# Sums of a folded Fourier transform on TensorE: eight 32-row, 64-column tiles of the array instead of four of 32 rows and 128 columns

## The chip, the cores and the metric

The kernel runs on one core of one Trainium2 chip. The metric is the device time of one execution in microseconds (us); runs are compared by their median. The profile is one execution of the program, recorded by the hardware profiler. Its engines: PE is the matmul side of TensorE and PEld its weight loads (a matmul keeps one operand, the weights, in the array and streams the other through it), DVE is VectorE, ACT is ScalarE, POOL is GpSimd, SP is SyncE, which only issues DMAs here.

## What is computed

The reference takes `x` of 8 batches, 3008 positions and 256 features, applies a Fourier transform along the positions and then the features, keeps the real part, and feeds every row to a gated feed-forward block with a sigmoid gate:

```
X = np.fft.fft(x, axis=1)
X = np.fft.fft(X, axis=2)
x = X.real.astype(np.float32).reshape(B * S, D)          # 24064 rows of 256
gate = 1.0 / (1.0 + np.exp(-(x @ w_gate)))               # w_gate, w_val: 256 x 1536
val = x @ w_val
return (gate * val @ w_out).astype(np.float32)           # w_out: 1536 x 256
```

All of it is in float32.

## The kernel before

**Stages.** The transform along the features is merged into the weights of the first two products (`merge`, lines 410 to 421). The transform along the positions is made per batch as sums over positions against tables of cosines and sines. Its two results per batch, `pk` and `qk` (128 features by 1505 frequencies), go through the feed-forward block in chunks of 252 frequencies: the matmuls `pf` (lines 774 to 792), the gate on ACT and DVE (lines 794 to 818), sums on POOL (line 824), the matmuls `po` (lines 857 to 896) and the way out (`finish`, line 898). The main loop (line 1151) runs over 8 batches x 6 chunks x 12 tiles of the hidden dimension. The order of everything is written out by hand: `at`, `mid`, `gap` and `spare` are lists that say behind which step of the main loop each piece of the next batch's transform stands.

**The transform of a batch.** Batch 0 uses whole columns of 128 rows (`half`, line 595). Batches 1 to 7 are folded further: by the symmetries of cosine and sine the positions are added and subtracted until a sum runs over a quarter of the rows. What is left are four groups of at most 32 rows, kept in the four quarters of the 128 partitions (`TILES`, line 198: a group `g`, a parity `par` and the first partition `lo`).

**`quarter(b, blk)`, lines 620 to 644**, makes the sums of one block of one batch. It runs 14 times: batches 1 to 7, blocks 1 and 0, from the list `mid` (lines 1093 and 1141). It takes four PSUM banks (`sum`, one for each group `t`). For each of two results (`what`), two parts (`part`) and three slices of rows (`q`), it calls `mm` for the four groups in turn: 48 calls. The weights of a call are 32 rows (31 at the end of some groups) by 128 columns of the folded input; the operand that is streamed is 32 rows by 95 columns (`NQ4`, line 197) of one of the tables `e4`, `r4` and `j4`. Each group starts on a partition of its own, so its call uses its own 32 rows of the array, and writes its own bank, at one of four ranges of 95 columns. Within a range the three slices `q` are added up in PSUM. `mm` (line 132) is a plain matmul with `start` and `stop` flags; the first call of a bank has `start`. All matmuls have line 133 in the profile, that of this helper; they are told apart by the tile they write: `sum` for these, `pf`, `po` and others for the rest. One float32 call of `mm` shows as two weight loads and two matmuls.

**Behind the sums**, ACT copies the four banks out, two copies a bank (line 644), and DVE makes the end results of them later (`quarter_ends`, line 646). The banks of `sum` are those of `po` (tags `po1` to `po4`), so the next matmuls of `po` in these banks wait for the copies. In the main loop `back` (line 1164) stands right ahead of the next matmuls after a `quarter`.

**Another user of parts of the array** is `e_sums` (lines 696 to 735): its matmuls `pe` have 128 rows and one or seven columns of weights, and write partitions 0, 32, 64 and 96 of one bank, so four of them use different columns of the array.

## Time and profile before

| | |
|---|---|
| median of 3 runs | 1908.67 us (1908.12 to 1909.44) |
| the profiled execution | 1909.15 us, span 1907.4 us |
| granted TensorE clock | 1.000 of full speed |
| busy PE, PEld | 1895.6 us, 1756.6 us |
| busy DVE, ACT, POOL | 1520.6, 1353.2, 1543.4 us |
| matmuls `pf`, two kinds | 4608, mean 376 ns each |
| matmuls `po`, two main kinds | 5528, mean 305 and 307 ns each |
| matmuls `sum` | 1344, median 270 ns each, and as many weight loads, median 187 ns |
| ACT copies of the sums (line 644) | 112, median 368 ns |

The span goes from the first to the last instruction; the time of the execution has some 1.7 us around it. Matmuls are pipelined: one lasts from its start to its last result, and the next can start long before that, so durations of one do not add up to busy time, and a busy PE is not one at its peak. In a timeline, neighbouring instructions of one kind are merged into a row: start, duration of all together, engine, line, kind, shapes and how many. A shape such as `32*128 32x95` says 32 rows and 128 columns of the array, and an operand of 32 partitions by 95 elements. In the rows by group, the numbers behind the first bar are busy time in us and the mean duration of one in ns; those behind the second, idle time of the engine ahead of them and what ended it. The chain that ended last is followed back from the last instruction: at each step to what released it, or to the instruction ahead of it on its engine.

### The profile page before, as it was taken

The numbers are of one execution on the slowest core, as the hardware profiler recorded it, in microseconds if no ns is written. First come the engines' busy times: TensorE is split into PE (matmuls) and PEld (weight loads), VectorE is DVE, ScalarE is ACT, GpSimd is POOL, SyncE is SP. The second block draws the span as 40 slices with busy tenths as digits, with TensorE's granted clock in tenths as the row PEclk, the third lists the DMA queues.
The fourth block names the chain that finished last, engine by engine and source line by source line (L and its number), as shares of the span: only waits on it lengthen the run. The fifth ranks groups of instructions, "written<-read, shape, count | busy, mean of one in ns | idle before, by whom it ended". The sixth has DMA issues, their size and how long they took to land.

```text
span 1907.4 us, 36057 instructions
## 1 busy us (share of the span) xinstructions
PE 1895.6 (99%) x11836; PEld 1756.6 (92%) x11836; DVE 1520.6 (80%) x3375; ACT 1353.2 (71%) x3235; POOL 1543.4 (81%) x2733
## 2 busy tenths in 40 slices
PE   8999999999999999999999999999999999999999
PEld 5788999999999999999999999999999999999998
DVE  7678888878979778897788878888788777977775
ACT  4777777777777777777777777677767777777775
POOL 2489879987999779997799878999789986877770
PEclk9999999999999999999999999999999999999999
DMA  8446221212022121211211212122120110010001
GB/s 315 120 134 80 71 89 51 72 33 81 21 64 54 31 87 32 62 41 37 89 39 48 45 39 81 40 52 58 30 74 17 36 37 15 15 25 17 15 18 30
DMA packets 197333, 109.33 MB, mean 57 GB/s; under 512 B 134823, under 2 KB 188818, under 8 KB 195354
## 3 DMA queue, kind: packets, MB, share of 16 engines
q1 hardware_dynamic: 196568, 106.50, 21.1%
q8 instruction: 95, 1.56, 0.3%
q14 instruction: 92, 0.75, 0.1%
q10 hardware_dynamic: 546, 0.51, 0.1%
q0 software_dynamic: 32, 0.00, 0.0%
HBM read 71.24 MB, written 47.87 MB: 62 GB/s over the span
## 4 chain that ended last, share of the span: by engine, by line
PE 94%; DMA 2%; SPq 1%; POOL 1%; ACT 1%; DVE 0%; issue 0%; ACTq 0%; POOLq 0%
PE pf L133 49%; PE po L133 41%; PE sum L133 2%; DMA rtab<-in_stab_dram 1%; PE ps L133 1%; POOL sf L824 1%; DMA st<-in_stab_dram 1%; SPq L206 1%; DMA raw<-in_moe_w_val_dram 0%; PE od L133 0%; POOL x L507 0%; SPq L192 0%; SPq L375 0%; PE pe L133 0%; PE ev L133 0%
## 5 line engine op out<-in xcount | busy, mean ns | idle before, releaser
L824 POOL TENSOR_TENSOR sf<-h,sf 128x168 f32<-128x168 f32 (+1 forms) x1104 | 621.0, 582 | 79.5 <-DVE h L818 75.9
L824 POOL TENSOR_TENSOR sf<-h 128x168 f32<-128x168 f32 (+1 forms) x920 | 519.3, 584 | 159.8 <-DVE h L818 158.0
L133 PE MATMUL pf<-qk,G 128*128 128x252 f32 (+1 forms) x2304 | 583.4, 376 | 0.9 <-ACT ae L787 0.8
L133 PE MATMUL pf<-pk,G 128*128 128x252 f32 (+1 forms) x2304 | 582.7, 376 | 0.0
L772 ACT ACTIVATE pf<-ek,ge 128x252 f32<-128x252 f32 (+1 forms) x1142 | 538.2, 471 | 23.2 <-DMA ge<-G 3.0
L133 PE MATMUL po<-sf,wf 128*128 128x168 f32 (+1 forms) x2944 | 508.3, 305 | 0.0
L787 ACT ACTIVATE ae<-pf 128x504 f32<-128x504 f32 (+1 forms) x576 | 338.8, 588 | 218.7 <-PE pf L133 217.2
L133 PEld LDWEIGHTS pf<-pk,G 128*128 128x128 f32 x2304 | 435.9, 190 | 53.3 <-ACT pf L772 1.5
L133 PE MATMUL po<-h,wf 128*128 128x168 f32 (+2 forms) x2584 | 461.3, 307 | 0.0
L133 PEld LDWEIGHTS po<-sf,wf 128*128 128x128 f32 x2944 | 453.4, 190 | 8.0
L818 DVE TENSOR_TENSOR h<-pf,z 128x252 f32<-128x252 f32 (+1 forms) x576 | 240.4, 417 | 274.0 <-ACT pf L815 270.5
L802 DVE TENSOR_TENSOR z<-ae,pf 128x504 f32<-128x504 f32 (+1 forms) x576 | 384.6, 668 | 83.1 <-ACT h L801 79.1
L908 DVE TENSOR_TENSOR c<-c 128x168 f32<-128x168 f32 (+1 forms) x920 | 438.7, 500 | 3.3
L133 PEld LDWEIGHTS pf<-qk,G 128*128 128x128 f32 x2304 | 410.6, 190 | 32.3 <-ACT ae L787 2.1
L133 PEld LDWEIGHTS po<-h,wf 128*128 128x128 f32 x2584 | 410.4, 190 | 17.8 <-issue 0.9
L801 ACT ACTIVATE h<-pf 128x252 f32<-128x252 f32 (+1 forms) x576 | 216.9, 376 | 146.3 <-PE pf L133 129.0
L815 ACT ACTIVATE pf<-z 128x252 f32<-128x252 f32 (+1 forms) x576 | 214.3, 372 | 116.4 <-DVE h L814 114.5
L814 DVE TENSOR_TENSOR h<-h,pf 128x252 f32<-128x252 f32 (+1 forms) x576 | 232.9, 404 | 0.0
L824 POOL TENSOR_TENSOR sf<-sf 128x168 f32<-128x168 f32 (+1 forms) x184 | 101.7, 553 | 14.4
L824 POOL TENSOR_TENSOR sf<-sf,h 128x168 f32<-128x168 f32 (+1 forms) x184 | 110.1, 598 | 0.0
L891 ACT COPY c<-po 128x504 f32<-128x504 f32 (+1 forms) x138 | 78.5, 569 | 0.0
L918 DVE STREAM_TRANSPOSE os<-c 128x256 f32<-128x256 f32 x188 | 76.5, 427 | 0.1
(158 smaller groups left out, 876.4 us busy)
## 6 DMA issues: line engine op xcount, KB each, us to landing
x<-xr SPq DMA_DIRECT2D x14, 1536.0 KB
out_dram<-os SPq DMA_DIRECT2D x376, 56.0 KB
xr<-in_xf_dram SPq DMA_DIRECT2D x105, 128.0 KB
x<-x SPq DMA_DIRECT2D x112, 96.0 KB
xr<-in_xf_dram SPq DMA_DIRECT2D x14, 384.0 KB
ek<-ed SPq DMA_DIRECT2D x40, 126.0 KB
out_dram<-os SPq DMA_DIRECT2D x288, 7.0 KB
xr<-in_xf_dram SPq DMA_DIRECT2D x21, 124.0 KB
```

The costliest lines, as they stand in the source:

```text
L133: nc.tensor.matmul(o, l, r, start=start, stop=stop, skip_group_check=True)
L772: nc.scalar.activation(PF[i][:, g], EK[i // NFT], AF.Copy, scale=ge[:, g, f : f + 1])
L787: nc.scalar.activation(AP[i], PF[i], AF.Copy, scale=2.0)
L801: nc.scalar.activation(H[p][:, fh, 0:n], PF[i][:, 0], AF.Sigmoid)
L802: nc.vector.tensor_tensor(z[:, :, ::-1], AP.pop(i), PF[i], op=ALU.subtract)
L814: nc.vector.tensor_tensor(h[:, fh, 0:n], h[:, fh, 0:n], pf[:, 1], op=ALU.mult)
L815: nc.scalar.activation(pf[:, 0], z[:, 0], AF.Sigmoid)
L818: nc.vector.tensor_tensor(h[:, fh, n:], pf[:, 0], z[:, 1], op=ALU.mult)
L824: nc.gpsimd.tensor_tensor(block(p, dst), block(p, a), block(p, b), op=(ALU.subtract, ALU.add)[op])
L891: (nc.vector.tensor_copy if t == 1 or t == 3 else nc.scalar.copy)(C[0][:, 3 * t * R : 3 * (t + 1) * R], PO[t][:, 0 : 3 * R])
L908: nc.vector.tensor_tensor(t[:, dst * R : (dst + 1) * R], *v, op=(ALU.subtract, ALU.add)[op])
L918: nc.vector.transpose(os_[0][0][:, s, 0:nb, h, :], t[:, c0 : c0 + nb * TB])
```

## The change

In `quarter`, each of the 48 calls becomes two. The first takes the weights' columns 0 to 63 and writes partitions 0 to 63 of the bank, the second takes columns 64 to 127 and writes partitions 64 to 127. Both stream the same 95 columns of the same table. The `start` and `stop` flags are as before, in each half. Nothing else is changed: the same banks, copies and places in the order.

```diff
                         c0 = (2 * what + 1 - part) * NQ4
-                        mm(ps[t][:, c0 : c0 + NQ4], W[b, blk][what][rows, w], tab,
-                           what == part == q == 0, q == N3 - 1)
+                        for at_ in (slice(0, HP), slice(HP, P)):
+                            mm(ps[t][at_, c0 : c0 + NQ4], W[b, blk][what][rows, w, at_], tab,
+                               what == part == q == 0, q == N3 - 1)
```

`HP` is 64 and `P` is 128. The halves of one group have the same rows of the array and different columns of it; with four groups they make eight tiles of 32 rows and 64 columns.

## The prediction, made before the result was known

> **What bounds the kernel now.** I read the busy shares first, then the chain that ended last, then the same chain around one of the stretches that the change touches.

> ```profile
> PE 1895.6 (99%) x11836; PEld 1756.6 (92%) x11836; DVE 1520.6 (80%) x3375; ACT 1353.2 (71%) x3235; POOL 1543.4 (81%) x2733
> ...
> PE 94%; DMA 2%; SPq 1%; POOL 1%; ACT 1%; DVE 0%; issue 0%; ACTq 0%; POOLq 0%
> PE pf L133 49%; PE po L133 41%; PE sum L133 2%; DMA rtab<-in_stab_dram 1%; PE ps L133 1%; POOL sf L824 1%; DMA st<-in_stab_dram 1%; SPq L206 1%; DMA raw<-in_moe_w_val_dram 0%; PE od L133 0%; POOL x L507 0%; SPq L192 0%; SPq L375 0%; PE pe L133 0%; PE ev L133 0%
> ```

> TensorE (PE) is the bound: 94% of the chain, no other engine over 81% busy. The sums of `quarter` are 2% of the chain, about 40 us, so that is all the change can work on. The chain in order of time near 220 us shows that a `quarter` is on it as a whole, between its neighbours on PE:

> ```profile
> 219.29 1.70 PE pf L133 x8
> 220.99 2.86 PE sum L133 x96
> 223.85 1.75 PE po L133 x10
> ```

> A microsecond saved or lost inside a `quarter` is therefore one in the total. There are 1344 matmuls of `sum` in the trace, 96 in each: 14 quarters (7 batches, two blocks). The code makes 48 calls of `mm` in each, so one float32 call is two loads and two matmuls.

> **What a quarter costs, and why.** The timeline of this quarter, whole and then its first instants (start, duration, how many):

> ```profile
> 220.92 2.77 PEld L133 LDWEIGHTS sum<-st,x 32*128 32x128 f32 x96 [0.33 <-DVE small L281]
> 220.92 2.93 PE L133 MATMUL sum<-st,x 32*128 32x95 f32 x96
> ```

> ```profile
> 220.92 0.36 PE L133 MATMUL sum<-st,x 32*128 32x95 f32 x4
> ...
> 220.92 0.20 PEld L133 LDWEIGHTS sum<-st,x 32*128 32x128 f32 x4 [0.33 <-DVE small L281]
> ```

> One load lasts 0.187 us and four last 0.20, so the four row tiles load side by side, some 7 ns apart. A quarter is then 24 rounds of four. The 96 loads take 2.77: 23 steps from round to round, the spread of four starts (0.02) and one load (0.187), so a step is (2.77 - 0.187 - 0.02) / 23 = 112 ns. What sets 112 ns? The groups by shape give the prices of one load and one matmul:

> ```profile
> L133 PEld LDWEIGHTS po<-sf,wf 128*128 128x128 f32 x2944 | 453.4, 190 | 8.0
> ...
> L133 PEld LDWEIGHTS po<-wl,h 128*116 128x116 f32 x24 | 4.3, 180 | 0.6
> ...
> L133 PEld LDWEIGHTS pe<-st,x 128*1 128x1 f32 x24 | 0.4, 81 | 1.3 <-issue 1.3
> ```

> ```profile
> L133 PE MATMUL pf<-qk,G 128*128 128x252 f32 x1920 | 487.1, 376 | 0.9 <-ACT ae L787 0.8
> ...
> L133 PE MATMUL po<-sf,wf 128*128 128x168 f32 x2496 | 432.2, 306 | 0.0
> ```

> A load is about 80 ns of latency and (190 - 81) / 127 = 0.86 ns a column, (190 - 180) / 12 = 0.83 at the upper end: 128 columns stream for 107 to 110 ns. A matmul streams (376 - 306) / 84 = 0.83 ns a column: 95 columns are 79 ns. The step of 112 is the load's stream and a few ns, not the matmul's. So the **weight loads** bound a quarter today, in each of the four row tiles, and the matmul leaves some 30 ns of every step unused.

> **The change, part by part.** Each call becomes two, one for the lower and one for the upper 64 columns of the weights, on the same 95 columns of the table.

> Added: 14 x 96 = 1344 matmuls and as many loads; a quarter has 192 pairs. A load is halved to 64 columns: 64 x 0.85 = 54 ns of stream, 58 with the same few ns. A matmul keeps its 79 ns, and 81 with its handover: four `pf` matmuls of 252 columns last 1.01 us in this timeline, so they start (1.01 - 0.376) / 3 = 211 ns apart, 2 more than 252 x 0.83 = 209.

> If the two halves run side by side as the row tiles do, a quarter is again 24 rounds, of eight pairs. A round takes the longer of load 58 and matmul 81: **81 ns** in place of 112. No row shows halves of 64 columns; the nearest is `pe`, four column tiles of all 128 rows:

> ```profile
> 24.61 0.50 PE L133 MATMUL pe<-st,x 128*1 128x377 f32 x4
> ```

> ```profile
> 24.61 1.44 PE L133 MATMUL pe<-st,x 128*1 128x377 f32 x16
> ```

> One lasts 0.478, four last 0.50, and sixteen last 1.44: rounds (1.44 - 0.478 - 0.02) / 3 = 314 ns apart, against 376 x 0.83 = 312 for one stream. So matmuls over the same rows and other columns go side by side, and the next loads are hidden below them, here of one column each.

> The unknown prices, from both sides. (a) The matmuls of two halves: side by side 81 a round, or one after the other 162. I take 81, by `pe`. (b) The loads of two halves, both from the same 32 partitions: side by side 58, or in turn 116. I take 58, by the loads that four row tiles share in 0.20 us; `pe` loads one to seven columns and can't say. (c) Handing 16 instructions to the array in each round: the first four loads and four matmuls begin within 0.02 us, under 4 ns each, while a whole quarter shows only 192 instructions in 2.7 us, 14 ns each. A round of 81 needs 5 ns each. I take it as hidden: the starts come in bunches of four with a pause after them, so the instructions stood waiting for the array and not the array for them. At 14 ns a quarter would take 384 x 14 = 5.4 us. A gain below 81 is excluded, as each tile still streams its 24 matmuls.

> The sum: 23 steps x (112 - 81) = 0.71 us a quarter. The first load is 54 ns shorter, and eight starts spread over 28 ns more than four; I let these cancel. 14 x 0.71 = **10 us less**.

> Costed at nothing, and their cover. What enters and leaves a quarter (a wait of 0.33 us ahead, the drain to `po` behind) happens as often as before. The eight ACT copies of line 644 can start 0.71 us earlier after each quarter; ACT sits idle before them in 13 of the 14, 14.0 us in all:

> ```profile
> who waited for it (us, times):
>   ACT st L644: 14.0, 13
> ```

> This is 1.08 us each, more than 0.71, so the copies keep their place behind PE; without that idle time PE would later wait up to 0.71 us for the banks that they empty, and the gain would be gone. No DMA is added but instruction fetches: 95 packets on that queue bring PE's program, of which 23672 are loads and matmuls, about 250 a packet, so 2688 more are 11 packets. A packet takes about 0.3% x 16 x 1907 / 95 = 1 us; a new quarter would use up 250 instructions in 1.3 us. That is cover, but thin.

> The profiled execution took 1909.15 us (span 1907.4), 0.5 over the median of 1908.67. 1909.15 - 10 = 1899.2, and from the median 1898.7. I write **1899**.

> [...]

> **Rivals.**

> 1. The loads of two halves go in turn: 116 a round, 4 x 23 x 14 = 1.3 us more, **1910**, no change to be measured. For it: one row tile loads at 0.85 ns a column today, and the 32 partitions that it reads stay the same. Against it: the row tiles' and `pe`'s side-by-side work.

> 2. Only four matmuls stream at a time, because halves of one row group exclude each other or because PE does not look far enough ahead in its program (the last of eight tiles is 28 instructions behind the first, and `pe` shows 15 at most). Eight matmuls take 162: (162 - 112) x 23 = 1.15 us, x 14 = 16 us slower, **1925**. Against it: `pe` as to columns; nothing as to reach.

> 3. The slow side by issue: PE's queue runs dry in a quarter, because 384 instructions can't be fetched and handed out at 5 ns. It decides from 7 ns an instruction (2.67 us / 384). At 10 ns: 3.84 us, 1.17 x 14 = 16 us, 1925; at the 14 of today's quarter 2.7 x 14 = 38 us, **1947**. For it: no stretch shows a rate above 14 for longer than a bunch, and a packet's 1 us against 1.3 us of work. Against it: the bunches. [...]

> 4. Loads wait for the matmuls of their own row group: two halves of 58 + 81 are 278 a round, 166 x 23 x 14 = 53 us slower, **1962**. The 112 of today speaks against it. [...]

> 5. PE gains and something else eats it (ACT's copies, above): at worst 14 x 0.71 back, 1909; it counts with rival 1.

> **How the numbers follow.** Forecast 0.48; rival 1 with 5: 0.15; rival 2: 0.17; rival 3: 0.18, of which 0.02 below 6 ns still faster, 0.03 about even, 0.13 slower; rival 4: 0.02. About 0.2% (3.8 us) is what a measurement of this kernel can tell from no change. Faster 0.50, same 0.15 + 0.03 = 0.18, slower 0.17 + 0.13 + 0.02 = 0.32. The forecast alone has 1896.5 to 1902 (rounds of 79 to 90). The range runs on over rivals 1 and 2 and rival 3 up to 10.5 ns: 1896.5 to 1928; outside are the rest of rival 3 (0.07), rival 4 and a few hundredths of the forecast.

> **What would show it.** Right: matmuls of `sum` x2688, 192 in some 2.2 us per quarter in the timeline, loads of 64 columns at about 134 ns, eight starts a round, PE's `sum` in the chain 2.1 us. Rival 1: rounds of 116. Rival 2: four starts, then 81 ns of none. Rival 3: starts of loads and matmuls evenly spread, loads idle for "issue" within a quarter. Wrong altogether: a quarter shortened but the total unmoved, with PE waiting for ACT line 644 behind it.

## The result, and the profile after

| | before | after |
|---|---|---|
| median of 5 runs | 1908.81 us (1908.12 to 1909.82) | 1918.30 us (1915.69 to 1920.99) |
| profiled execution, span | 1909.15, 1907.4 us | 1920.99, 1919.2 us |
| mean granted clock of it | 1.000 | 0.997 |

The changed kernel is **slower** by half a percent: 1.0049 times the time of before (95% interval 1.0034 to 1.0064), 9.5 us by the medians. The forecast was 10 us faster. Its runs are also spread wider, 5.3 us against 1.7.

From the page of the changed kernel, the lines that answer to those shown of before:

```profile
PE 1898.5 (99%) x13180; PEld 1757.3 (92%) x13180; DVE 1518.3 (79%) x3375; ACT 1353.4 (71%) x3235; POOL 1544.0 (80%) x2733
...
q8 instruction: 105, 1.72, 0.4%
...
PE 96%; POOL 1%; DMA 1%; issue 1%; DVE 0%; SPq 0%; ACT 0%; ACTq 0%; POOLq 0%
```

PE is the bound as before. New is 1% of "issue" on the chain: time in which an engine waited for nothing that the profile shows. The instruction queue brought 105 packets in place of 95. The chain in order of time around the first quarter shows where that 1% is:

```profile
218.20 1.70 PE pf L133 x8
219.90 2.17 PE sum L133 x129
222.07 2.04 issue
224.11 0.59 PE sum L133 x32
224.70 2.05 PE po L133 x10
226.75 2.95 PE pf L133 x8
```

PE works through 160 of the 192 pairs, stands still for 2 us in the middle of its own program, and then does the last 32. Behind it another thing is new: eight `pf` matmuls take 2.95 us where they took 1.70 just before. The windows of the same stretch (busy time of PE, PEld, DVE, ACT, POOL; then the granted clock, DMA share and GB/s) show the clock halved there:

```profile
215.00:219.00 4.00, 4.00 (x24) 3.63 (x23) 2.88 (x8) 3.93 (x10) 3.92 (x10) 1.00 0.31 65
221.90:224.00 2.10, 0.17 (x13) 0.00 (x0) 1.89 (x6) 0.79 (x3) 1.79 (x4) 1.00 0.89 276
225.75:229.05 3.30, 3.30 (x11) 2.82 (x10) 0.17 (x1) 1.21 (x5) 0.48 (x1) 0.50 0.57 125
```

The DMA engines are busy during this stall (share 0.89), but a stall does not need that: from 922.07 to 925.48 us, the stretch with the stall of the eighth quarter, the share is 0.00.

Not every quarter stalls. This is the second one, in the timeline of PE:

```profile
263.79 2.60 PE L133 MATMUL sum<-st,x 32*64 32x95 f32 x192
266.32 1.66 PE L133 MATMUL po<-h,wf 128*128 128x164 f32 x10
```

It takes 2.60 us against 2.93 before, a gain of 0.33 where 0.71 was forecast. And how many stall, from the list of waits (who waited for what: us in all, times, longest):

```profile
PEld sum L133 <- issue: 11.0, 7, 2.2
```

An eighth stall stands just behind the third quarter, among the matmuls of `po`:

```profile
419.08 0.84 PE L133 MATMUL po<-h,wf 128*128 128x168 f32 x4
420.69 0.98 PE L133 MATMUL po<-h,wf 128*128 128x168 f32 x5 [0.77 <-issue]
```

**Where the 9.5 us come from.** 14 quarters gain 0.33 each: 4.6 us less. Seven of them stall, 11.0 us (11.4 counted from the start of the instruction ahead of the stall to the start of the one behind it, "from start to start" below), and 0.8 behind an eighth: 11.8 us more. The records of the granted clock have three stretches of 3.41 us at half speed, at 225.7, 925.5 and 1389.7 us, each within 2 us after the end of a stall; in the kernel before it stayed at full speed from 8.8 us to 1906.7. Half speed for 3 x 3.41 us costs 5.1 us at most. The sum, 11.8 + 5.1 - 4.6 = 12.3, stands against the difference of the two profiled executions, 1920.99 - 1909.15 = 11.8. The run of the changed kernel with the clock at 1.000 throughout took 1915.69, 6.9 over the median of before: 11.8 - 4.6 = 7.2. So the number of these clock dips, which differs from run to run, accounts for most of the spread: the three runs at 0.999 (one dip, by the same working) took 2.3 to 3.1 us more than the one at 1.000, and the profiled one with three dips took 5.3 more, where a dip costs 1.7 at most.

**A pattern in the stalls.** Counting PE's instructions in order of time through the trace (loads, matmuls and PE's own waits), the first instruction behind each of the seven stalls inside a quarter has the same place modulo 256: 193. PE's program comes in 105 packets of 16 KB, and the 27043 instructions counted are 257 a packet, so this is taken for the end of such a piece. Each quarter has 384 instructions and so contains one or two ends. How far into the quarter the first end lies decides:

| first end, instructions into the quarter | stall, us |
|---|---|
| 19, 41 | 0.55, 1.19, at the second end |
| 63, 64, 74, 96, 118 | 1.83, 2.28, 1.78, 1.93, 1.89, at the second end |
| 1, 2 | none (second end at 257, 258) |
| 136 | the one of 0.8 behind the quarter (second end at 392, the quarter has 384) |
| 158, 180, 213, 235 | none |

From this the **supply theory**, the author's reading of these places: the packet for the piece after next starts at about the time when an end is passed, and is there some time later; if PE gets through the 256 instructions in between sooner, it stands still. In the changed kernel the packets start between 3.75 us ahead of such a pass and 9.6 us behind it, with a median of 0.8 behind. Why an end at 1 or 2 brings no stall and one at 19 does is taken up at the end of the experiments. Before, 192 instructions in 2.7 us never did that.

### The profile page after: what moved, and what is told of

Its sections match the earlier page's. It is cut to its first block, busy times and chain, and to the rows that moved or that the text cites. A ratio compares the mean times of both kernels' runs of the same rounds, so it can differ in the third digit from the quotient of the medians.

```text
span 1919.2 us, 38745 instructions
## 1 busy us (share of the span) xinstructions
PE 1898.5 (99%) x13180; PEld 1757.3 (92%) x13180; DVE 1518.3 (79%) x3375; ACT 1353.4 (71%) x3235; POOL 1544.0 (80%) x2733
## 4 chain that ended last, share of the span: by engine, by line
PE 96%; POOL 1%; DMA 1%; issue 1%; DVE 0%; SPq 0%; ACT 0%; ACTq 0%; POOLq 0%
PE pf L133 50%; PE po L133 42%; PE sum L133 2%; PE ps L133 1%; POOL sf L825 1%; DMA st<-in_stab_dram 0%; DMA raw<-in_moe_w_val_dram 0%; PE od L133 0%; POOL x L507 0%; SPq L192 0%; SPq L375 0%; PE pe L133 0%; PE ev L133 0%; DVE c L909 0%; DVE z L803 0%
## 5 line engine op out<-in xcount | busy, mean ns | idle before, releaser
L133 PE MATMUL pf<-qk,G 128*128 128x252 f32 (+1 forms) x2304 | 585.8, 377 | 0.3 <-ACT ae L788 0.2
L133 PE MATMUL pf<-pk,G 128*128 128x252 f32 (+1 forms) x2304 | 583.6, 376 | 0.0
L133 PE MATMUL po<-sf,wf 128*128 128x168 f32 (+1 forms) x2944 | 508.3, 305 | 0.0
L133 PEld LDWEIGHTS pf<-pk,G 128*128 128x128 f32 x2304 | 437.2, 190 | 53.5 <-ACT pf L773 1.4
L133 PE MATMUL po<-h,wf 128*128 128x168 f32 (+2 forms) x2584 | 463.4, 308 | 0.8 <-issue 0.8
L133 PEld LDWEIGHTS po<-sf,wf 128*128 128x128 f32 x2944 | 453.3, 190 | 8.0
L133 PEld LDWEIGHTS pf<-qk,G 128*128 128x128 f32 x2304 | 412.3, 191 | 31.7 <-issue 2.0
L133 PEld LDWEIGHTS po<-h,wf 128*128 128x128 f32 x2584 | 411.7, 191 | 19.0 <-issue 1.9
```

What stands on the lines that cost most here:

```text
L133: nc.tensor.matmul(o, l, r, start=start, stop=stop, skip_group_check=True)
```

## The experiments

Times are medians unless one run is told of; each group was run beside the kernel before, whose medians were 1909.1 to 1909.7.

**e1 and e2: move the ends of the pieces.** Tiny matmul calls, four PE instructions each, are put behind the four warm-up calls, 30 in e1 (shown) and 62 in e2; every end then falls 120 or 248 instructions earlier in the work.

```diff
     for i in range(4):
         mm(warm[:, 0:WC], dt[:, 0, 0:P], dt[:, 0], True, True)
+    for i in range(30):
+        mm(warm[0:TB, 0:TB], dt[:, 0, 0:TB], dt[:, 0, 0:TB], True, True)
```

> The changed kernel with 30 tiny matmul calls (120 PE instructions) put ahead of everything, at the warm-up. Supply theory: PE's program comes in pieces of 256 instructions and a quarter stalls where it crosses two ends of pieces; counted from the trace, every stall of the changed kernel stands at the same place in its piece (193 of 256). So the stalls move: five of the 14 quarters stall (the 3rd, 6th, 7th, 10th and 11th, after 16, 93, 38, 115 and 60 plus 256 instructions), and the seven that stalled before do not, bar none; sum of the stalls about 7 us, the time 3 to 7 us over the kernel before. Rival, something that happens at that point of the work (a transfer, a late engine): the 1st, 4th, 5th, 8th, 9th, 12th and 13th quarter stall as before, and the time stays 9 to 10 us over.

Measured: 1916.58, ratio 1.0036 (1.0022 to 1.0050), 6.9 us over the kernel before; the profiled execution 5.4 over, clock 1.000. The first quarter, which had the longest stall, in the timeline of PE, and the sixth, which had none:

```profile
221.36 2.86 PE L133 MATMUL sum<-st,x 32*64 32x95 f32 x192
...
686.94 2.42 PE L133 MATMUL sum<-st,x 32*64 32x95 f32 x174
691.08 0.48 PE L133 MATMUL sum<-st,x 31*64 31x95 f32 x18 [1.73 <-issue]
```

The 3rd, 6th, 7th, 10th and 11th quarter stall and no other, each again at 193 of 256, 0.74, 1.97, 0.37, 1.77 and 1.67 us from start to start. None of the seven of the changed kernel is among them. A sum for it: 6.5 of stalls, some 2 behind quarters (the list of waits has 2.0 for `po`), 0.8 for the tiny calls by e3's 1.6 for 248, less 4.6, is 4.7 against 5.4. What the work is at that point does not matter; where the program is cut does.

> The same with 62 calls (248 PE instructions). Supply theory: nine quarters stall, the seven of the changed kernel and also the 2nd and the 14th, these two by little (0.3 us); sum about 12 us, the time 7 to 12 us over the kernel before. Rival: the seven of the changed kernel alone.

Measured: 1921.61, ratio 1.0066 (1.0051 to 1.0081). The list of waits:

```profile
PEld sum L133 <- issue: 12.7, 9, 2.2
```

Nine quarters, the nine named, the 2nd and 14th with 0.65 and 0.56 us, more than the 0.3 expected. The three dips of the clock are there as well.

**e3: control.** The 62 tiny calls in the kernel before.

> Control: the kernel before with the same 248 tiny instructions. Both theories: no stall in any quarter, each as long as before (2.93 us of matmuls), and the time within 2 us of the kernel before, which is the price of the tiny matmuls.

Measured: 1911.31, ratio 1.0008 (0.9998 to 1.0017), all quarters 2.66 us from first to last start as before, and no dip of the clock. So the ends alone do not bring stalls, and the denser program is needed too; the tiny calls cost 1.6 us by the medians (up to 3.2 by the interval).

**e4: the array alone.** The upper half of the sums is left out, which leaves half of the pairs and as many instructions as before.

```diff
-                        for at_ in (slice(0, HP), slice(HP, P)):
+                        for at_ in (slice(0, HP),):
...
-                nc.scalar.copy(to, ps[t][:, ...
+                nc.scalar.copy(to[0:HP], ps[t][0:HP, ...
```

> The changed kernel with the upper 64 columns of the weights left out: 96 pairs of 64 columns a quarter, as many instructions as the kernel before, and the copies move the lower half alone (the upper half of the sums is left out). Load-bound theory (a step of 112 ns is the stream of 128 columns of weights): rounds of 82 ns all the way, a quarter's matmuls 2.2 us in place of 2.93, no stalls, the time about 1899. Rival, that the 112 ns is how fast PE hands out the 192 instructions: rounds stay near 112 and the time near 1908.

Measured: 1900.22 in one run beside 1909.69, and in the timeline of PE:

```profile
221.35 2.21 PE L133 MATMUL sum<-st,x 32*64 32x95 f32 x96
223.49 0.98 PE L133 MATMUL po<-h,wf 128*128 128x168 f32 x5
```

0.72 us less than 2.93 in each quarter, 14 x 0.72 = 10 us; the total fell by 9.5. Halving the columns of a load takes away the bound that the 112 ns were read as, and a saving inside a quarter reaches the end.

**e5: halves apart.** Why does a quarter without a stall take 2.60 and not 2.2? First another order of the calls.

```diff
-                for q in range(N3):
+                for q, at_ in itertools.product(range(N3), (slice(0, HP), slice(HP, P))):
                     for t, (g, par, lo) in enumerate(TILES):
...
-                        for at_ in (slice(0, HP), slice(HP, P)):
-                            mm(ps[t][at_, ...
+                        mm(ps[t][at_, ...
```

> The changed kernel with another order of its calls: for each slice the four lower halves, then the four upper ones. The same 384 instructions a quarter, so the same seven quarters stall. What is in question is the length of a quarter that doesn't stall, 2.4 us from first to last start where rounds of 82 ns would give 2.0. If the pace is that of handing out instructions (6 ns each), it stays at 2.4. If it is lost because two calls for the same rows stand next to each other in the program, it falls towards 2.0.

Measured: 1916.04 in one run; the second quarter again takes 2.60 us, and the same seven stall at the same places. Calls for the same rows side by side in the program are not what costs.

**e6: less to stream.** 48 columns in place of 95; the other columns of the sums are left out, and the copies move 48.

```diff
-                            mm(ps[t][at_, c0 : c0 + NQ4], W[b, blk][what][rows, w, at_], tab,
+                            mm(ps[t][at_, c0 : c0 + 48], W[b, blk][what][rows, w, at_], tab[:, 0:48],
```

> The changed kernel streaming 48 columns of each table in place of 95 (the other columns of the sums are left out, and the copies move 48). The array needs 58 ns a round then (loads of 64 columns), 1.4 us a quarter. If instructions are handed out at a fixed pace of 6 ns, a quarter that doesn't stall stays near 2.3 us; if the loss follows the array's own times, it falls to about 1.7. The supply theory also has each stall a few tenths longer if the quarter gets faster, at the same places (193 of 256).

Measured: 1921.02 in one run (four dips of the clock), and the second quarter:

```profile
264.84 2.21 PE L133 MATMUL sum<-st,x 32*64 32x48 f32 x192
```

2.0 us from first to last start, between the two expectations. In the trace the first 64 instructions go at 4.0 ns each, 64 ns a round against the 58 worked out ahead, and the next 256 at 5.3. With 95 columns the same counts are 5.5 and 6.1. Neither reading holds alone: behind the first 64 the instructions came at one in 5.3 ns even with half of the columns, and at 6.1 with all 95 a part of the rounds took over 100 ns where 81 were forecast; how, stays open. The stalls are longer in all seven quarters, by 0.05 to 0.8 us from start to start (the longest is 3.0), and an eighth has 0.17.

**e10: six tiles.** Two groups keep both halves, two keep the lower one; the sums of the others are left out.

```diff
-                        for at_ in (slice(0, HP), slice(HP, P)):
+                        for at_ in (slice(0, HP), slice(HP, P))[0 : 2 - g]:
```

> The changed kernel without the upper halves of two of its four groups: six tiles, 288 instructions a quarter (a quarter of the sums is left out, with the copies of it). Two groups still have both their halves. Array-bound, a quarter without a stall takes 24 rounds of 82 ns, 2.0 us. If the 2.4 us of eight tiles come from halves of a group getting in each other's way, the two whole groups still do so and it stays near 2.4. If they come from the supply, which has to bring 32 instructions for every 164 ns, 24 for the same time are within its reach and it is 2.0.

Measured: 1900.62 in one run beside 1909.06, no stall in any quarter, and

```profile
220.49 2.27 PE L133 MATMUL sum<-st,x 32*64 32x95 f32 x144
```

2.27 us against 2.21 of e4. Two halves of a group run side by side at nearly the full pace when fewer instructions are needed for the same time. So the 2.60 of eight tiles do not come from halves that disturb each other. The number of instructions remains as the likelier cause; a loss that sets in only when eight tiles work at a time would look the same in e10 and is not excluded.

**e8: time between two ends.** Other work that stands behind the quarter is put between its two results: `between` is the call `front_b(i)`, four matmuls of `pf` in the trace.

```diff
         for what in range(2):
+            if what:
+                between()
```

> The changed kernel with four matmuls of pf (front_b, 0.85 us) between the two halves of each quarter (what 0 and what 1), so that no more than 192 instructions come at full speed. If what counts is the time from one end of a piece to the next (some 3.5 us are needed, by the distance from the first end to the restart in the stalled quarters), the stalls shrink by about 1.2 us each and those under 1.2 us vanish: sum of stalls about 4 us in place of 11. If what counts is only that two ends fall in a quarter, the stalls keep their lengths. Two more changes of tiling a quarter cost about 0.2 us each way, 14 x 0.2 to 0.4 = 3 to 6 us; time 1910 to 1915.

Measured: 1914.76 in one run. The first quarter in the timeline of PE:

```profile
219.81 1.44 PE L133 MATMUL sum<-st,x 32*64 32x95 f32 x96
221.18 1.12 PE L133 MATMUL pf<-qk,G 128*128 128x252 f32 x4
222.23 1.01 PE L133 MATMUL sum<-st,x 32*64 32x95 f32 x60
224.65 0.78 PE L133 MATMUL sum<-st,x 32*64 32x95 f32 x36 [1.41 <-issue]
```

The stalls of the same seven quarters sum to 4.5 us from start to start in place of 11.4 (1.65, 0.54, none, 1.00, 0.25, 0.65, 0.45); they shrink by 0.55 (all of it) to 1.4 us each, where the other work takes 1.2 us. The one of 1.19 left 0.25, though it was expected to vanish. So it is the time between two ends that counts, and not only that two fall into a quarter. The clock stayed at 1.000.

**e7 and e9: eight tiles where they fit.** The ends can be computed ahead, so each quarter gets eight tiles or four by where they fall. e9 is e7 with two tiny calls (8 instructions) behind the warm-up.

```diff
+EIGHT = ((1, 0), (2, 0), (3, 1), (4, 1), (4, 0), (5, 0), (6, 1), (7, 1), (7, 0))
...
+        eight = (b, blk) in EIGHT
...
-                        for at_ in (slice(0, HP), slice(HP, P)):
+                        for at_ in (slice(0, HP), slice(HP, P)) if eight else (slice(0, P),):
```

> Eight tiles in nine of the 14 quarters, those in which no two ends of pieces fall, and four tiles as before in the other five. Supply theory: no stall in any quarter, the granted clock at 1.000, nine quarters shorter by 0.33 us each: 3.0 us less than the kernel before, about 1906. Rival, that eight tiles cost something behind the quarter too, or that stalls come with a count of instructions in a time and not with these places: no gain or a loss, 1909 to 1914.

Measured: 1907.12 against 1909.13, ratio 0.9989 (0.9980 to 0.9998), clock 1.000. Thirteen quarters do as expected; the 13th still stalls, and `po` behind the fifth stands still for 0.67 us at an end:

```profile
1565.26 1.81 PE L134 MATMUL sum<-st,x 32*64 32x95 f32 x127
1567.86 1.05 PE L134 MATMUL sum<-st,x 31*64 31x95 f32 x65 [0.79 <-issue]
```

> The kernel of e7 with two tiny calls (8 PE instructions) ahead of everything. In e7 one quarter, the 13th, still stalled (1.0 us): an end of a piece fell on the instruction just ahead of it and the next 256 later, inside. Eight instructions move every end eight places earlier, out of the 13th quarter's reach. Supply theory: no stall in any of the 14 quarters, nine of them 0.3 us shorter, so 2.7 to 3 us less than the kernel before, about 1 us less than e7. Rival, that e7's last stall has to do with that quarter's work: it stays, and the time with it.

Measured: 1907.61 against 1909.06, ratio 0.9992 (0.9983 to 1.0001). The expectation failed: the 13th quarter stalls again (0.91 us from start to start), now with the earlier end nine instructions ahead of it, and again at 193 of 256; `po` behind the fifth has 0.43. In both kernels the packet that goes with that earlier end begins 0.1 us after the quarter does; in quarters at a like distance from an end that do not stall it begins 0.65 to 1.4 us ahead of it. Why it is later there is open. The gain of e7 and e9 is 1.5 to 2 us of 1909, at the edge of what can be told.

**The packets themselves.** The traces hold the start of every packet of PE's program. In each of the twelve kernels there are as many packets as places 193 modulo 256, so they can be paired in order, each packet with the place after its own number (with the place of its own number it would come up to 9.9 us too late). In none of them does a piece's first instruction start less than 2.27 us after its packet does, and the 44 stalls inside a quarter all end 2.28 to 3.04 us after it. So PE is taken to wait for the packet. The start of the packet for the second end moves with the first end: in the changed kernel it lies 0.8 us ahead of the quarter's start with the first end at 1 or 2, and 0.75 to 1.8 us behind it with the first end at 41 to 136. This fits the rows of the table that the distance alone leaves open: with the first end at 1 or 2 PE reaches the second one 2.35 or 2.31 us after the packet's start, without a stall; with the first end at 19 the packet starts 0.3 us ahead, and the stall ends 2.55 us after it. What sets the start of a packet to within a microsecond is not shown.

## Why the prediction was wrong

**Right.** PE as the bound, and a saving in a quarter reaching the end (e4: 9.5 of 10 us). The weight load as what sets the 112 ns (e4). Halves of a row group side by side: the first 16 loads of the changed kernel last

```profile
219.83 0.23 PEld L133 LDWEIGHTS sum<-st,x 32*64 32x64 f32 x16 [0.33 <-DVE small L281]
```

in all, one of them 0.13, so rivals 1 and 4, with loads in turn, are out. From one eighth start of a matmul to the next the second quarter has a first step of 132 ns and then 22, of which 15 take 81 to 92 ns, where 81 was forecast; the 162 of rival 2 are nowhere. The copies behind a quarter (line 645 now) do not hold PE up: the list of waits of the changed kernel names none of PE for them.

**The step that failed** is unknown price (c), handing 16 instructions to the array in each round: "I take it as hidden". It was taken from the bunches of four in a program at 14 ns an instruction, which show how close together four can start (under 4 ns), and say nothing of a pace kept up over 384. The runs showed two limits in its place: a pace of 5 to 6 ns an instruction at which the other 7 of those 22 steps take 101 to 130 ns, so that the round of the sum, 81 ns, is 96 on the average and 0.71 us a quarter became 0.33 (e6 and e10; how the steps are lost is open), and pieces of 256 that cost up to 2.3 us where two ends lie too close in time (e1, e2, e8). The prediction had both numbers of the second, 1 us a packet against 1.3 us for 250 instructions, and called it cover, "but thin". The packet's own time of 1 us is not the whole wait: in the seven stalls PE goes on 2.3 to 2.7 us after the packet's start.

Rival 3 named this mechanism and its sign, loads idle for "issue" within a quarter. Its price was wrong in form: a steady rate over all quarters, not a few long stalls that depend on where a piece ends. Its other sign, starts evenly spread, is seen in part, in the quarters without a stall too: behind the first 32 loads, which come in bunches of eight, most follow one another 4 to 17 ns apart. In the second quarter the 192 matmuls start within 2.60 - 0.24 = 2.36 us, 12 ns apart. The half-speed clock after a stall, up to 5.1 us of the profiled 11.8, was in no part of the prediction.

## What to carry to other kernels

Count instructions, not only array time: splitting a matmul into more tiles multiplies loads and matmuls (1344 of `sum` became 2688 of each), and here PE began no piece of 256 instructions sooner than 2.27 us after its packet's start, while a quarter of eight tiles works through 256 in about 1.5 us (two ends in quarters without a stall). An idle time put down to "issue" in the middle of PE's dense stretch, at the same place modulo 256 each time, was here a program that arrived too late; moving it with some tiny instructions ahead of everything (120 in e1) told this apart from a cause in the work at that point. Six tiles in place of eight nearly kept the array's pace (2.27 against 2.21 us) and did not stall.
